# Attention's probabilities times values: 64 matmuls of one head, or 32 of two heads against block-diagonal values

## Chip, cores and metric

The kernel runs on one core of a Trainium2 chip. The metric is the time of one execution on the device, in microseconds (us), as the median of several runs. Durations of single instructions come from one profiled execution.

## What is computed

Two blocks, A (attention) and B (a gated MLP with a mix over positions), are applied twice, with the same weights. S is 2048, D is 576, there are 32 heads of 18.

```python
def _A_ref(x, wqkv, wo):                       # H = 32, Dh = 18, W = 8, dil = 2
    q, k, v = heads of (x @ wqkv)
    idx = pos[:, None] - off[None, :]          # off = 0, 2, ..., 14: eight keys, every second row back
    logits = where(idx >= 0, q . k[idx] * Dh ** -0.5, -1e9)
    o = softmax(logits) @ v[idx]
    return o (heads side by side) @ wo

def _B_ref(x, w_in, w_sp, b_sp, w_out):
    z1, z2 = halves of gelu(x @ w_in)
    g = w_sp @ layernorm(z2) + b_sp
    return (z1 * g) @ w_out

x = A_x
x = x + _A_ref(layernorm(x));  x = x + _B_ref(layernorm(x))
x = x + _A_ref(layernorm(x));  x = x + _B_ref(layernorm(x))
```

## The kernel before

Five phases follow one another. `phase_F(0)` normalizes x, does the first attention and the second half of the MLP's input projection. `phase_S(1)` does the first half of that projection and the mix over positions (`g_ps`). `phase_F(2)` first multiplies by `w_out` (`p_ps`), then does the second attention and projection as in the first; `phase_S(3)` mixes again and `phase_E` writes the result. The text calls `phase_F(0)` and `phase_F(2)` the first and second F stage. They hold all that the change touches.

Attention goes in 18 tiles of 114 queries with a halo of 14 rows before them. Since keys lie two rows apart, a tile's 128 rows are split by parity: 64 even and 64 odd rows never meet, and 57 queries of one parity see 64 keys of the same. For a tile t the steps are:

- `v{t}.m` (PE, 20 matmuls, `v_ps`): x times the value weights, 16 matmuls on 128x64 tiles of the array, 4 on 64x64 tiles for the last 64 of the 576 input features. Output rows are one parity each. `v{t}` copies the result, on ACT or DVE, into one of three buffers `v_ext`, which have a column of ones behind each head's 18.
- `a{t}.La`, `a{t}.L` (PE, 64 matmuls, `L_ps`): the scores, per head and parity 64 keys by 57 queries, four tiles of the array side by side.
- `a{t}.x0`, `.x1` (ACT): exp into `P`. `a{t}.k` (DVE) masks it.
- `a{t}.v` (PE, 64 matmuls, `O_ps`, L639), called PV below: for each head and parity the stationary operand is P, 64 keys by 64 (57 queries and 7 of padding), the moving one the head's 18 values and its one. Each sits on a 64x64 tile of the array.
- `a{t}.f` (DVE, L647 and L648): divide by the sum that the ones gave. Then `.t` (PE transpose, `o_tp`), `.e` (copy out), and per 128 rows the output projection `w_ps` (L695), the residual, a layernorm (its transposes are `ln_tp`, L325) and the MLP's projection `z_ps`.

The queries and keys come from `qk_ps` (45 matmuls for two tiles) and go through DRAM (`qk_bounce`) to get heads onto partitions.

Each F stage collects its steps in a `Flow`. A planner sorts them at build time: each step has an engine, a cost in us, a key, predecessors, and the buffers that it takes. PSUM tiles of two banks carry the tag "H", of which there are three, shared by `v_ps`, `L_ps`, `O_ps`, `qk_ps`, `w_ps`, `p_ps` and `z_ps`; a buffer is free again when the last step that uses it ends. The planner's order is then written into each engine's queue, and each engine works through its queue in that order. A step's `mode` names the way in which PE's array is tiled ("w" whole, "c" 128x64, "h" 64x64, "q" scores, "n" 64 rows); a step whose mode has two letters can begin in the one and end in the other. `pairs` counts a step's matmuls, with which the planner keeps a model of the fetching of PE's instructions. Keys and model have constants in `PLANS`, one `Plan` for each F stage.

```python
fl = Flow(dict(H=3, PT=2, QK=3, bn=2, stg=6, xt=NX, xn=3, ln_st=6, o_t=2), pl.STAY, self.pairs, pl.LF)
```

Of the kernel before, what the change touches and what calls it, by code (L numbers as in the profile page):

```python
# [18 lines left out]
P = 128  # L19
# [28 lines left out]
PLANS = (Plan(LX=4, LW=3.41, LR=3.7, KQ=4.43, KX=11.27,  # L48
              KV=1.9, KL=2.12, KE=20.8, KM=1.4, KP=2.05, KF=11.96, KY=2.1, KZ=15.77, KS=0.81, STAY=0.73, LF=4.38),
         Plan(LX=5.14, LW=3.5, LR=4.76, KQ=4.3, KX=10.56,  # L50
              KV=1.51, KL=1.98, KE=2.03, KM=0.75, KP=0.52, KF=4.06, KY=4.27, KZ=15.86, KS=0.39, STAY=0.48, LF=3.89))
# [140 lines left out]
class K:  # L192
# [219 lines left out]
    def phase_F(self, li):  # L412
# [14 lines left out]
        vb = [pool.tile([P, H, DH + 1], bf16, name=f"v_ext{k}") for k in range(3)]  # L427
        wqk = pool.tile([P, NM, 2 * D], bf16, name="wqk")
        wqk_r = pool.tile([P, D + HP], bf16, name="wqk_r")
        wv = pool.tile([P, NM, 2, 288], bf16, name="wv")  # L430
        wv_r = pool.tile([P, 288], bf16, name="wv_r")
# [45 lines left out]
        def load_v():  # L477
            self.load576(lambda s: wv[:, :, s, :], wv_r, self.A_wqkv[:, 2 * D:2 * D + 288],
                         self.A_wqkv[:, 2 * D + 288:3 * D], (nc.gpsimd if first else nc.sync,))
# [92 lines left out]
        def V_steps(t, key):  # L572
            box, v = {}, vb[t % 3]

            def mm(rest_first):
                ps = box["ps"] = self.Ht("v_ps")
                c0 = QT * t

                def part(first, wide):
                    for c in range(NM) if wide else (NM,):  # L580
                        for s in range(2):
                            rows = slice(0, P) if wide else slice(HP * s, HP * s + HP)
                            for par in range(2):
                                self.read_xn_strided(nc.tensor.matmul(  # L584
                                    ps[HP * (par ^ s):HP * (par ^ s) + HP, s, 0:288],
                                    lhsT=self.xnD[rows, c, c0 + par:c0 + P:2], rhs=wv[:, c, s, :] if wide else wv_r[rows, :],
                                    start=(first and c in (0, NM)), stop=(not first and c in (NM - 1, NM)),
                                    tile_position=(rows.start, HP * (par ^ s))), c0, c0 + P)
                part(True, not rest_first)
                part(False, rest_first)  # L590

            def ev(e):
                self.copy(e, v[:].rearrange("p (s b) d -> p s b d", s=2)[:, :, :, 0:DH],
                          box["ps"][:, :, 0:288].rearrange("p s (b d) -> p s b d", d=DH))
# [6 lines left out]
        def ATT_steps(t, key):  # L601
# [5 lines left out]
            def Lm(a):  # L607
                def f(_):
                    qk = self.QKs[group[t]]
                    ps = box["L", a] = self.Ht("L_ps")  # L610
                    for g in range(8):
                        for par in range(2):
                            for j in (2 * a, 2 * a + 1):
                                rows = slice(32 * j, 32 * j + DH)
                                at = HP * (par ^ (g // 4))
                                nc.tensor.matmul(ps[at:at + HP, j % 2, g * QH:(g + 1) * QH],  # L616
                                                 lhsT=qk[rows, g, 1, par, kb:kb + HP],
                                                 rhs=qk[rows, g, 0, par, kb + HALO // 2:kb + HALO // 2 + QH],
                                                 start=True, stop=True, tile_position=(32 * j, at))
# [13 lines left out]
            def pv(_):  # L633
                O = box["O"] = self.Ht("O_ps")
                for h in range(H // 2):
                    for s in range(2):
                        for par in range(2):
                            rows, to = slice(HP * (par ^ s), HP * (par ^ s) + HP), slice(HP * par, HP * par + HP)
                            nc.tensor.matmul(O[to, s, h * (DH + 1):(h + 1) * (DH + 1)],  # L639
                                             lhsT=Psb[rows, h % 4, h // 4 + 4 * s, :], rhs=v[rows, h + 16 * s, :],  # L640
                                             start=True, stop=True, tile_position=(rows.start, to.start))

            def fin(_):
# [14 lines left out]
            fl.step(tag + ".v", "PE", 0.75, key - pl.KP, pv, [tag + ".k", f"v{t}"] + ([f"a{t - 1}.v"] if t else []),  # L658
                    takes=[("H", tag + ".O")], mode="h", pairs=2 * H)
# [113 lines left out]
        def fills(part):  # L773
            if part == 0:
                for k in range(2):
                    nc.gpsimd.memset(Pb[k][:, :, :, QH:HP], 1.0)
                for k in range(3):
                    nc.gpsimd.memset(vb[k][:, :, DH:DH + 1], 1.0)
# [10 lines left out]
        fl.step("wo", q0, 1.2, -17, lambda _: load_o(), ["wv", "qk1"] if first else [], lag=4.0)  # L789
        fl.step("wzero", "POOL", 0.3, -19, lambda _: nc.gpsimd.memset(wqk_r[HP:P, NM * P:NM * P + P], 0.0))  # L790
        fl.step("fills", "POOL", 1.8, -16, lambda _: fills(0), ["wv", "lnx6.p"] if first else [])
# [185 lines left out]
```

## Time and profile before

| | us |
|---|---|
| runs | 1237.36, 1231.66, 1235.93 |
| median | 1235.93 |
| profiled execution | 1232.45 |
| its span, first to last instruction | 1230.8 |
| first F stage ends (first matmul of `phase_S(1)`) | 230.3 |
| second F stage (from its first `p_ps` to the first matmul of `phase_S(3)`) | 550.9 to 834.5 |

In rows of the profile, "PEld" is TensorE's load of a stationary operand and "PE" its matmul; "x64" is a count. A row of the timeline has its start and length in us, and in brackets how long the engine sat idle before it and what ended that. Consecutive instructions of a kind are merged, and a row's length reaches to the end of the last one's pipeline, so from one row's start to the next row's is the better measure of what a group costs.

### The profile page before, as it was taken

To read this page: it belongs to the slowest core of one execution; us is meant where nothing else is said; L and a number is where in the kernel's file an instruction comes from. 1 tells how busy PE (TensorE), PEld (TensorE's weight loads), DVE (VectorE), ACT (ScalarE), POOL (GpSimd) and SP (SyncE) were. 2 spreads that over 40 slices of the span, in tenths; PEclk is the share of its full clock that TensorE was granted. 3 is DMA by queue.
4 is the path that set the end of the run, shared out by engine and by line. 5 is a ranking of instruction groups with operands and counts; after the bars stand their busy time and mean duration, and the time that the engine had idled before them with its cause. 6 is when DMAs were issued, how large, how long until landed. Compare 5 with 4: busy or idle time off the path is not lost.

```text
span 1230.8 us, 27537 instructions
## 1 busy us (share of the span) xinstructions
PE 1195.9 (97%) x12032; PEld 680.9 (55%) x12094; DVE 531.5 (43%) x873; ACT 390.3 (32%) x667; POOL 198.9 (16%) x484
## 2 busy tenths in 40 slices
PE   6999999999999999999999999999999999999998
PEld 4676655444444444448777776554444444444576
DVE  6677765333232232333466666553232332232311
ACT  6664787510111111003344657772111001111000
POOL 6210267400000000002111114672000000000000
PEclk9999999999999999999999999999999999999999
DMA  7654346340000000032322362009300000000121
GB/s 201 131 131 118 75 96 133 75 96 2 10 10 10 10 11 1 1 108 86 74 62 57 92 160 56 17 22 263 94 10 10 1 10 10 10 1 29 40 68 49
DMA packets 140202, 75.09 MB, mean 61 GB/s; under 512 B 96576, under 2 KB 137216, under 8 KB 140080
## 3 DMA queue, kind: packets, MB, share of 16 engines
q1 hardware_dynamic: 139392, 70.94, 24.5%
q0 software_dynamic: 688, 2.38, 0.7%
q8 instruction: 95, 1.56, 0.6%
q14 instruction: 27, 0.22, 0.1%
HBM read 39.40 MB, written 17.11 MB: 46 GB/s over the span
## 4 chain that ended last, share of the span: by engine, by line
PE 93%; issue 2%; DMA 1%; ACT 1%; DVE 1%; SPq 1%; POOL 0%; ACTq 0%; POOLq 0%
PE g_ps L888 40%; PE p_ps L362 11%; PE z_ps L288 10%; PE z_ps L864 8%; PE qk_ps L288 5%; PE v_ps L584 4%; PE w_ps L695 3%; PE z_bank L864 3%; PE z_ps L282 2%; PE L_ps L616 2%; PE O_ps L639 2%; PE ln_tp L325 1%; PE z_ps L870 1%; PE qk_ps L282 1%; PE o_tp L667 1%
## 5 line engine op out<-in xcount | busy, mean ns | idle before, releaser
L888 PE MATMUL g_ps<-W,zu 128*128 128x512 bf16 x2256 | 497.7, 379 | 2.5
L888 PEld LDWEIGHTS <-zu 128*128 128x128 bf16 x2304 | 225.4, 98 | 271.8
L893 DVE TENSOR_TENSOR g_tmp<-g_ps,bsp 128x512 f32<-128x512 f32 x144 | 98.9, 687 | 432.9 <-PE g_ps L888 432.9
L880 ACT ACTIVATE zu<-z_ps 128x1024 bf16<-128x1024 f32 x54 | 51.4, 1024 | 515.9 <-PE z_ps L870 508.5
L362 PEld LDWEIGHTS <-zu 128*128 128x128 bf16 x1152 | 111.9, 98 | 31.0 <-DVE zu L894 2.1
L288 PE MATMUL z_ps<-wA,xnD 128*128 128x384 bf16 x576 | 109.8, 327 | 0.1
L362 PE MATMUL p_ps<-wA,zu 128*128 128x288 bf16 x768 | 105.9, 286 | 0.5 <-DVE ob L407 0.5
L894 DVE TENSOR_TENSOR zu<-g_tmp,zu 128x512 bf16<-128x512 f32 x144 | 99.6, 692 | 10.8
L288 PEld LDWEIGHTS <-xnD 128*128 128x128 bf16 x768 | 70.6, 98 | 56.2 <-issue 14.8
L864 PE MATMUL z_ps<-xnD,w 128*128 128x512 bf16 x424 | 95.8, 378 | 0.4
L864 PEld LDWEIGHTS <-w 128*128 128x128 bf16 x576 | 54.3, 97 | 71.8 <-issue 7.9
L732 ACT ACTIVATE zu<-z_ps 128x768 bf16<-128x768 f32 x96 | 77.2, 804 | 33.3 <-PE z_ps L288 17.4
L742 DVE CUSTOM_DVE_ANT_1 zu<-zu 128x1536 bf16<-128x1536 bf16 x32 | 56.6, 1770 | 49.1 <-ACT zu L732 49.1
L288 PE MATMUL qk_ps<-xnD,wqk 128*128 128x242 bf16 x576 | 73.4, 275 | 3.2 <-issue 2.1
L624 ACT ACTIVATE P<-L_ps 128x912 bf16<-128x912 f32 x72 | 64.7, 946 | 15.9 <-PE L_ps L616 14.4
L288 PEld LDWEIGHTS <-wqk 128*128 128x128 bf16 x576 | 54.0, 100 | 15.6 <-issue 9.5
L308 POOL TENSOR_SCALAR ln_st<-ln_st 128x1 f32<-128x1 f32 x64 | 15.4, 241 | 277.5 <-DVE ln_st L304 237.9
L319 ACT ACTIVATE xn<-zu,ln_st 128x512 bf16<-128x512 bf16 (+1 forms) x56 | 33.4, 647 | 66.0 <-POOL ln_st L310 65.7
L790 POOL MEMSET wqk_r<- 64x128 bf16 x2 | 0.4, 198 | 308.4 <-issue 308.4
L319 ACT ACTIVATE xn<-xt,ln_st 128x512 bf16<-128x512 bf16 x72 | 42.7, 648 | 20.1 <-POOL ln_st L310 20.0
L695 PE MATMUL w_ps<-wo,oT 128*128 128x288 bf16 x320 | 46.1, 293 | 2.7 <-ACT P L624 1.4
L288 PE MATMUL z_ps<-wB,xnD 128*128 128x384 bf16 x192 | 46.9, 326 | 0.0
(86 smaller groups left out, 1121.9 us busy)
## 6 DMA issues: line engine op xcount, KB each, us to landing
qk_bounce<-stg SPq DMA_DIRECT2D x72, 121.0 KB
QK<-qk_bounce SPq DMA_DIRECT2D x72, 121.0 KB
w<-in_B_w_in_dram SPq DMA_DIRECT2D x36, 128.0 KB
wA<-in_B_w_in_dram SPq DMA_DIRECT2D x12, 288.0 KB
wA<-in_B_w_out_dram SPq DMA_DIRECT2D x4, 864.0 KB
xres<-xt SPq DMA_DIRECT2D x18, 144.0 KB
x<-xres SPq DMA_DIRECT2D x16, 144.0 KB
out_dram<-ob SPq DMA_DIRECT2D x15, 144.0 KB
```

The costliest lines, as they stand in the source:

```text
L288: nc.tensor.matmul(ps(s), lhsT=lhsT, rhs=rhs, start=(c == 0 and not rest_first), stop=(c == NM - 1 and rest_first))
L319: nc.scalar.activation(out=out, in_=in_, func=ACT.Identity, scale=rstd[:n], bias=nmr[:n])
L362: nc.tensor.matmul(ps[:, hh, 0:288], lhsT=u[:, s * S + i * P:s * S + (i + 1) * P], rhs=wout(b, s)[:, hh * 288:(hh + 1) * 288], start=(b == ...
L624: nc.scalar.activation(out=Psb[:, 2 * hh:2 * hh + 2, :, 0:QH], in_=box["L", hh][:, :, 0:8 * QH].rearrange("p a (b c) -> p a b c", c=QH), f ...
L695: nc.tensor.matmul(box["ps"][:, hh, 0:288], lhsT=oT[:, c, at:at + P], rhs=wo[:, c, hh * 288:(hh + 1) * 288], start=(c == 0), stop=(c == 4))
L732: nc.scalar.activation(out=self.zu[:, 3 * u:3 * u + 3, 256 * i:256 * (i + 1)].rearrange("p j (s r) -> p s j r", s=2), in_=box[u][:, :, 0:3 ...
L742: nc.vector.tensor_tensor_reduce(out=junk(0, 6), in0=z[:, 0:6, :], in1=z[:, 0:6, :], scale=1.0 / FH, scalar=0.0, op0=ALU.mult, op1=ALU.add ...
L864: nc.tensor.matmul(out[q][h], lhsT=w1[:, NM * h + c, :], rhs=self.xnD[:, c, PADL + 512 * q:PADL + 512 * q + 512], start=(first and c == 0) ...
L880: nc.scalar.activation(out=uq, in_=H3[q][:], func=ACT.Gelu_apprx_tanh)
L888: nc.tensor.matmul(ps[:, s, :], lhsT=z2[:, i, s, :], rhs=W[q][:, i, :], start=(i == 0), stop=(i == NS - 1))
L893: nc.vector.tensor_tensor(out=tmp[:], in0=ps[:, s, :], in1=bsp[:, 512 * q:512 * (q + 1)], op=ALU.add)
L894: nc.vector.tensor_tensor(out=uv, in0=tmp[:], in1=uv, op=ALU.mult)
```

## The change

One PV matmul now takes two heads. Its stationary operand is P on all 128 rows, 64 keys of one head above 64 keys of another, same parity; its moving operand has 38 columns, 19 for each head, with zeros where the rows are the other head's (`v_ext` is block-diagonal and twice as wide). A matmul covers a 128x64 tile of the array, and there are 32 a tile instead of 64. For that

- the scores are written so that two heads of one parity lie above one another; their matmuls come in another order, number and size unchanged;
- `v_ps` has the even rows' heads and the odd rows' arranged anew (the weights are read as two runs of 144 columns), and is copied out in two steps of 64 rows, `v{t}.e0` and `v{t}.e1`, in place of one of 128 rows; PV waits for both;
- the three `v_ext` are zeroed at the start of each F stage (`vzero0` to `vzero2`, on DVE in the first, on POOL in the second), and the step `fills` waits for that;
- the value weights come in three DMAs in place of four;
- PV is entered in the planner with 0.45 us and 32 matmuls, not 0.75 and 64, and as mode "c", not "h"; the constants in `PLANS` are others, and so the order of all steps in both F stages is computed anew.

```diff
-PLANS = (Plan(LX=4, LW=3.41, LR=3.7, KQ=4.43, KX=11.27,
-              KV=1.9, KL=2.12, KE=20.8, KM=1.4, KP=2.05, KF=11.96, KY=2.1, KZ=15.77, KS=0.81, STAY=0.73, LF=4.38),
-         Plan(LX=5.14, LW=3.5, LR=4.76, KQ=4.3, KX=10.56,
-              KV=1.51, KL=1.98, KE=2.03, KM=0.75, KP=0.52, KF=4.06, KY=4.27, KZ=15.86, KS=0.39, STAY=0.48, LF=3.89))
+PLANS = (Plan(LX=4, LW=3.41, LR=3.7, KQ=4.95, KX=12.29,
+              KV=2.02, KL=2.15, KE=22.44, KM=1.86, KP=2.02, KF=13.34, KY=2.53, KZ=15.66, KS=0.73, STAY=0.73, LF=4.38),
+         Plan(LX=5.14, LW=3.5, LR=4.76, KQ=4.29, KX=10.53,
+              KV=0.36, KL=2.04, KE=1.11, KM=0, KP=0.18, KF=6.22, KY=4.16, KZ=15.99, KS=0.47, STAY=0.73, LF=3.89))
...
-        vb = [pool.tile([P, H, DH + 1], bf16, name=f"v_ext{k}") for k in range(3)]
+        vb = [pool.tile([P, 2, H // 2, 2, DH + 1], bf16, name=f"v_ext{k}") for k in range(3)]
...
             def ev(s):
+                def f(e):
+                    rows = slice(HP * s, HP * s + HP)
+                    self.copy(e, v[rows, :, :, s, 0:DH], box["ps"][rows, :, 0:288].rearrange("p r (h d) -> p r h d", d=DH))
+                return f
...
-            fl.step(f"v{t}", ("ACT", "DVE"), dict(DVE=0.78, ACT=0.66), key, ev, [f"v{t}.m"], [f"v{t}.ps"])
+            for s in range(2):
+                fl.step(f"v{t}.e{s}", ("ACT", "DVE"), dict(DVE=0.78, ACT=0.66), key, ev(s), [f"v{t}.m"], [f"v{t}.ps"])
...
-                    for g in range(8):
+                    for g in (0, 2, 1, 3, 4, 6, 5, 7):
...
-                                at = HP * (par ^ (g // 4))
-                                nc.tensor.matmul(ps[at:at + HP, j % 2, g * QH:(g + 1) * QH],
+                                at, to = HP * (g // 2 % 2), 4 * par + 2 * (g // 4) + g % 2
+                                nc.tensor.matmul(ps[at:at + HP, j % 2, to * QH:(to + 1) * QH],
...
-                for h in range(H // 2):
-                    for s in range(2):
+                for h in range(8):
+                    for b in range(2):
                         for par in range(2):
-                            rows, to = slice(HP * (par ^ s), HP * (par ^ s) + HP), slice(HP * par, HP * par + HP)
-                            nc.tensor.matmul(O[to, s, h * (DH + 1):(h + 1) * (DH + 1)],
-                                             lhsT=Psb[rows, h % 4, h // 4 + 4 * s, :], rhs=v[rows, h + 16 * s, :],
-                                             start=True, stop=True, tile_position=(rows.start, to.start))
+                            to = slice(HP * par, HP * par + HP)
+                            nc.tensor.matmul(O[to, b, 0:16 * (DH + 1)].rearrange("p (s h e) -> p s h e", s=2, h=8)[:, :, h, :],
+                                             lhsT=Psb[:, h % 4, 4 * par + 2 * b + h // 4, :], rhs=v[:, par, 8 * b + h],
+                                             start=True, stop=True, tile_position=(0, to.start))
...
-            fl.step(tag + ".v", "PE", 0.75, key - pl.KP, pv, [tag + ".k", f"v{t}"] + ([f"a{t - 1}.v"] if t else []),
-                    takes=[("H", tag + ".O")], mode="h", pairs=2 * H)
+            fl.step(tag + ".v", "PE", 0.45, key - pl.KP, pv, [tag + ".k", f"v{t}.e0", f"v{t}.e1"] + ([f"a{t - 1}.v"] if t else []),
+                    takes=[("H", tag + ".O")], mode="c", pairs=H)
...
+        vz = "DVE" if first else "POOL"
+        for k in range(3):
+            fl.step(f"vzero{k}", vz, 0.7 if first else 1.2, -21, lambda _, k=k: (nc.vector if first else nc.gpsimd).memset(vb[k][:], 0.0))
```

More of the change, by code (lines that the diff above doesn't have):

```diff
@@ L426, in phase_F @@
         wo = pool.tile([P, 5, D], bf16, name="wo")
-        vb = [pool.tile([P, H, DH + 1], bf16, name=f"v_ext{k}") for k in range(3)]
+        vb = [pool.tile([P, 2, H // 2, 2, DH + 1], bf16, name=f"v_ext{k}") for k in range(3)]
         wqk = pool.tile([P, NM, 2 * D], bf16, name="wqk")
         wqk_r = pool.tile([P, D + HP], bf16, name="wqk_r")
-        wv = pool.tile([P, NM, 2, 288], bf16, name="wv")
-        wv_r = pool.tile([P, 288], bf16, name="wv_r")
+        wv = pool.tile([P, NM, 2, 2, 144], bf16, name="wv")
+        wv_r = pool.tile([P, 2, 2, 144], bf16, name="wv_r")
         oT = pool.tile([P, 5, RING], bf16, name="oT")
@@ L477, in load_v @@
         def load_v():
-            self.load576(lambda s: wv[:, :, s, :], wv_r, self.A_wqkv[:, 2 * D:2 * D + 288],
-                         self.A_wqkv[:, 2 * D + 288:3 * D], (nc.gpsimd if first else nc.sync,))
+            eng = nc.gpsimd if first else nc.sync
+            self.dma(wv[:].rearrange("p c b s n -> p c (b s n)"),
+                     self.A_wqkv[0:NM * P, 2 * D:3 * D].rearrange("(c p) n -> p c n", p=P), eng)
+            for r in range(2):
+                self.dma(wv_r[HP * r:HP * r + HP].rearrange("p b s n -> p (b s n)"), self.A_wqkv[NM * P:D, 2 * D:3 * D], eng)
         def load_o():
@@ L777, in fills @@
                 for k in range(3):
-                    nc.gpsimd.memset(vb[k][:, :, DH:DH + 1], 1.0)
+                    for s in range(2):
+                        nc.gpsimd.memset(vb[k][HP * s:HP * s + HP, :, :, s, DH:DH + 1], 1.0)
                 nc.gpsimd.memset(wo[0:HP, 4, :], 0.0)
```

16 lines of the change are left out of this document (8 added, 8 removed).

## The prediction

> **What bounds the kernel now.** I read the page first, then who PE waited for, then stretches and the order of time around PE's longest pauses.
>
> ```profile
> PE 1195.9 (97%) x12032; PEld 680.9 (55%) x12094; DVE 531.5 (43%) x873; ACT 390.3 (32%) x667; POOL 198.9 (16%) x484
> q8 instruction: 95, 1.56, 0.6%
> ```
>
> PE is busy 97% of the span, so only two things can move the end: work that PE no longer does, and pauses of PE that go or come. The second row is the queue that brings instructions: 95 packets and 1.56 MB, 16.4 KB a packet. PE has 12032 + 12094 = 24126 instructions on the first row; 95 packets make 254 for each packet, about 127 pairs of a weight load and a matmul. The view of PE's waits shows what its pauses are:
>
> ```profile
> PE O_ps L639 <- issue: 4.1, 3, 2.0
> PE v_ps L584 <- issue: 3.8, 5, 1.8
> PE qk_ps L288 <- issue: 2.1, 3, 1.0
> PE w_ps L695 <- ACT P L624: 1.4, 1, 1.4
> PE L_ps L616 <- ACT P L624: 0.9, 1, 0.9
> PE L_ps L616 <- issue: 0.9, 1, 0.9
> PE O_ps L639 <- DVE zu L407: 0.7, 1, 0.7
> ```
>
> The figures are us in total, times, and the longest. "Issue" is a wait for nothing that the profile shows. The four such rows make 10.9 us; the w_ps row, 1.4, is put down to an exp that doesn't feed `w_ps`, so I count it with them: 12.3 us in all. The order of time from one pause to the next, PE alone, shows where they fall:
>
> ```profile
> 99.92 0.68 PE L639 MATMUL O_ps<-v_ext,P 64*64 64x19 bf16 x64
> 100.47 0.32 PE L584 MATMUL v_ps<-wv_r,xnD 64*64 64x288 bf16 x4
> 100.72 1.78 PE L584 MATMUL v_ps<-wv,xnD 128*64 128x288 bf16 x26
> 103.28 0.56 PE L584 MATMUL v_ps<-wv,xnD 128*64 128x288 bf16 x6 [0.77 <-issue]
> 103.77 0.32 PE L584 MATMUL v_ps<-wv_r,xnD 64*64 64x288 bf16 x4
> 104.02 0.70 PE L616 MATMUL L_ps<-QK 18*64 18x57 bf16 x64
> 104.65 0.45 PE L667 MATMUL o_tp<-ident,o_t 128*128 128x128 bf16 x5
> 104.94 0.44 PE L325 MATMUL ln_tp<-ident,xn 128*128 128x128 bf16 x5
> 105.22 0.99 PE L288 MATMUL qk_ps<-xnD,wqk 128*128 128x242 bf16 x8
> 106.14 0.38 PE L282 MATMUL qk_ps<-xnD,wqk_r 64*128 64x242 bf16 x4
> 106.46 1.83 PE L288 MATMUL qk_ps<-xnD,wqk 128*128 128x242 bf16 x16
> 108.22 0.28 PE L282 MATMUL qk_ps<-xnD,wqk_r 64*128 64x242 bf16 x2
> 108.43 1.23 PE L639 MATMUL O_ps<-v_ext,P 64*64 64x19 bf16 x128
> 109.49 0.31 PE L584 MATMUL v_ps<-wv_r,xnD 64*64 64x288 bf16 x4
> 109.74 0.81 PE L584 MATMUL v_ps<-wv,xnD 128*64 128x288 bf16 x10
> ```
>
> Both pauses cut a V step in its middle (26 and 10 matmuls in), where no operand is missing. From 103.28 to the second pause stand 6+4+64+5+5+8+4+16+2+128+4+10 = 256 matmuls: two packets exactly. Stretches between ends of pauses (length, PE's busy time and matmuls, granted clock, DMA) say the same:
>
> ```profile
> 40.03:44.94 4.91, 3.86 (x127) 1.00 0.43 136
> 44.94:49.58 4.64, 3.76 (x127) 1.00 1.03 154
> 725.02:741.33 16.31, 14.18 (x382) 1.00 0.61 154
> ```
>
> 127, 127 and 382 (three times 127). So PE pauses where a packet of its own program ends and the next isn't there; starved, it gets one packet in 4.64 to 4.91 us. I call such a packet a block of 128 matmuls. Elsewhere a block holds 128 long matmuls and the fetch is hidden; in attention it can hold 2 us of work.
>
> The Trainium skill, in "Runtime: NRT & Kernel Launch" (Instruction fetch mechanics), has the instruction memory refilled in 16 KiB blocks of 256 instructions, and calls the cost of crossing a block mostly hidden. The trace agrees on the block (254) and disagrees on the cost (12.3 us); by that rule the next part's first two terms would be nothing, a rival below.
>
> Two pauses have an aftermath. The granted clock (the figure behind the matmuls) after them:
>
> ```profile
> 112.20:115.62 3.42, 3.24 (x19) 0.50 0.02 5
> 132.68:136.10 3.42, 3.19 (x14) 0.50 0.46 88
> ```
>
> Half the clock for 3.42 us costs 1.7 us twice, 3.4 us. Pauses of the fetch thus cost 12.3 + 3.4 = 15.7 us, all in the two F stages.
>
> **The change part by part.**
>
> *Fewer instructions.* PV has 64 matmuls a tile and gets 32; 36 tiles lose 1152 pairs, 9 blocks. What counts is the blocks that hold too little work. I price a matmul by the rows above, from its start to the next group's start: scores 0.63/64 us, PV 1.06/128, V (0.25 for four, 1.78/26 for the rest) 0.067 on average, transposes 0.0575, projection 0.92/8. The output projections, 128 columns of weights and 288 of data, come from
>
> ```profile
> 554.00 1.63 PE L362 MATMUL p_ps<-wA,zu 128*128 128x288 bf16 x12
> 555.47 0.90 PE L362 MATMUL p_ps<-wB,zu 128*128 128x288 bf16 x6
> ```
>
> as 1.47/12 = 0.1225. With these prices I go through the order in which each kernel's PE instructions are built, in blocks of 128, and add up what each block lacks to 4.64 us. I do it for four places where the first block may begin and average. Before: 17.7 us lacking in the first F stage and 20.7 in the second, 38.4; after, with PV at double the price a matmul, 7.6 and 8.3, 15.9; with PV at the old price 19.7. That is no time, since blocks fetched ahead make up for part of it, but the ratio is what I use: 0.41 of the lack stays (0.51 at most), so of 12.3 us of pauses 5.1 stay: **-7.2 us** (bounds: nothing, if the pauses have another cause, and -12.3). No long pause, no half clock: two windows of 1.7 us; I expect three quarters to go, **-2.5** (0 to -3.4).
>
> *PV itself.* 1.06 us for 128 matmuls is 0.53 a tile. Four array tiles of 64x64 work side by side, so 16 rounds of 33 ns. The new matmuls cover 128 rows, so only two (left and right 64 columns) stand side by side: 32 matmuls are again 16 rounds. What sets a round? Not the data: 57 columns in the scores (0.63/64, four tiles as well) cost 39 ns a round against 33 for 19. It looks like the load of 64 weight columns, and that doesn't depend on rows:
>
> ```profile
> L584 PEld LDWEIGHTS <-xnD 128*64 128x64 bf16 x576 | 30.7, 111 | 11.2 <-issue 6.7
> L639 PEld LDWEIGHTS <-P 64*64 64x64 bf16 x2304 | 22.2, 109 | 9.2 <-issue 7.1 <-DVE P L631 0.2 <-DVE stg L342 0.2
> ```
>
> 111 ns for 128 rows against 109. So a PV step stays near 0.53. If a matmul costs 8.3 ns wherever it runs, it falls to 0.27: 36 x 0.26 = -9.4 us. If load and 38 data columns didn't overlap in a tile, a round grows by the 38 columns (1.78/26 for 288 columns in two tiles is 137 ns a round, so 18 ns): 16 x 18 ns x 36 = +10 us. The V steps, with the same 128x64 tiles, do overlap (137 ns a round with a load in it). I take **-0.9**, by the scores' and V's rows. Changes of tile size on PE are as many in the new order (179 in the first stage; 179 against 186 in the other).
>
> The skill's "TensorEngine Tiling (Array Packing)" (Instruction Overhead) says that a matmul of one column takes as long as one of 60. The rows lean to it (39 against 33 ns). By itself it would make half the matmuls half the time, but it leaves out that half the tiles stand side by side; the sum by it is the second rival.
>
> *Two evacuations of V for one.* Each takes 64 rows, but 576 elements in each row as the whole did, so I give each the whole's time. Copies, then busy times of PE, its loads, DVE, ACT and POOL in two stretches:
>
> ```profile
> L343 ACT CAST v_ext<-v_ps x28: 627/641/653, 25.4 to 758.5; 128x576 bf16<-128x576 f32 x28
> L342 DVE CAST v_ext<-v_ps x8: 707/759/760, 24.0 to 747.1; 128x576 bf16<-128x576 f32 x8
> 35.00:150.00 115.00, 106.17 (x3014) 81.77 (x3012) 83.09 (x150) 69.50 (x106) 19.36 (x44) 0.97 0.52 118
> 575.00:785.00 210.00, 202.66 (x4011) 151.83 (x4009) 129.50 (x233) 117.17 (x193) 50.87 (x122) 1.00 0.33 76
> ```
>
> The built order gives DVE 33 halves for 8 wholes (25 x 0.76 = 19 us more) and ACT 39 for 28 (11 x 0.64 = 7 us more). DVE has 115 - 83 = 32 us free in the first attention stretch and gets 16 halves there, 12 us; the other stretch has 80 free on DVE, 93 on ACT. So the work has room. The price is lateness: `v_ps` holds one of three "H" slots until both halves are out, and PV now waits for both. Behind a late half on PE stand the next score or projection matmuls that need the slot; the mask and the normalization on DVE stand behind the copy. I take **+2.5** (0 to 25, if each tile's half were in PE's way).
>
> *Zeroing the values.* Three memsets of 1216 bf16. In the first stage on DVE ahead of the first statistics:
>
> ```profile
> 0.91 0.09 DVE L226 MEMSET xnD<- 128x35 uint32 x1
> 0.95 0.07 DVE L227 MEMSET xnD<- 128x10 uint32 x1
> 3.06 0.46 DVE L303 BATCH_NORM_STATS2 ln_st<-zu 128x6 f32<-128x288 bf16 x1 [2.05 <-DMA zu<-in_A_x_dram]
> ```
>
> 25 words more cost 0.02 us; 608 words then 0.55 us, three 1.65, inside the 2.05 that DVE waits for x: **0**. Were it per bf16 element (1.04 each), 1.1 us would stick out, straight on the path to the first matmul. In the second F stage POOL does them ahead of its layernorm steps, under the p_ps matmuls (rows of 554 us) that come first: 0. The value weights come by one DMA less on POOL's and SP's queues; rows and x loads behind it go up by an issue, nothing on the path: 0.
>
> *Scores and V matmuls* keep number, size and tiles; scores visit the same two tiles twice running, then the other two. With loads pulled ahead that costs nothing; the V weights are read in two runs of 144: 0.
>
> **Sum.** 1232.45 (profiled execution, span 1230.8) - 7.2 - 2.5 - 0.9 + 2.5 = 1224.3. The timed median, 1235.93, is 3.5 above the profiled execution; I add half of that and forecast **1226 us**. Its own range is 1220 (the other pauses and their half clock gone too, 5.1 and 0.9) to 1232 (half of the gain on pauses fails, 3.6, and the evacuations cost 2.5 more).
>
> **The rivals.**
>
> *PV halves as well.* 8.3 ns is then a cost of each matmul. For it: 39 ns against 33 with thrice the columns, so columns count little. Against: rounds with few tiles (V) show no gain from fewer matmuls. 1226 + 0.9 - 9.4, and 1.2 back because blocks get emptier: 1219. Chance 0.15.
>
> *The pauses aren't worth anything.* Crossing a block is hidden by other work, or the pauses move to other places of the new order; the first two terms vanish: 1226 + 9.7 = 1236, no change. The skill's rule of the fetch is this case. Against it: counts of 127, 256 and 382. Chance 0.15, with PV at +10 us in it (1236 too).
>
> *The second half of V's evacuation is in PE's way.* In-order ACT and DVE put it behind an exp or a mask; PE lacks a slot. From (7.2 + 2.5 + 0.9)/36 = 0.29 us a tile on, the change loses; at 0.70 a tile (the mean of 0.64 and 0.76) it is 25 us: 1226 - 2.5 + 25 = 1248.5, slower. For it: DVE goes from 83 to 95 of 115 us in the first stretch. Against: in the waits above ACT and DVE hold scores and PV up by 0.9 and 0.7 us in all. Chance 0.22.
>
> **How the numbers follow.** The forecast has 0.48. A measurement of this kernel can tell about 0.5% from no change, here 6.2 us: below 1229.8 is faster, above 1242.1 slower. Of the forecast's 0.48 I put 0.43 below 1229.8, with 0.15 of the first rival: 0.57 with rounding. No change: 0.05, 0.13 of the second rival, little of the third: 0.20. Slower: 0.23. The range, 1213 to 1246, reaches from the first rival with its other pauses gone (0.51 x 12.3 = 6.3 us) to the third at 0.63 us a tile.
>
> **What would show it.** Right: the instruction queue has some 86 packets (95 - 9); PE's waits on "issue" at O_ps, v_ps, qk_ps and L_ps make 5 us or less; no window at half clock in attention; a PV step of 32 starts its successor 0.5 us on. Wrong: PV at 0.27 or 0.8 us a step; pauses of PE that DVE or ACT end, in rows of O_ps, L_ps and qk_ps, of over 10 us; pauses on "issue" as long as before.

## The result, and the profile after

The changed kernel takes 1226.88 us, median of 6 runs (1225.88 to 1229.43), beside 1233.14 for the kernel before (1230.36 to 1237.36, also 6): ratio 0.9939, 95% interval 0.9918 to 0.996. It is faster by some 6 us. The profiled execution took 1226.56 us, its span 1224.8. From the page of after, the engines' busy times and the queue that brings instructions:

```profile
PE 1196.8 (98%) x10942; PEld 679.3 (55%) x10942; DVE 551.4 (45%) x894; ACT 396.8 (32%) x683; POOL 200.4 (16%) x492
...
q8 instruction: 86, 1.41, 0.5%
```

86 packets, as forecast. PE's busy time hardly moved (1195.9 before, where 62 matmuls are missing in the records: 12094 loads, 12032 matmuls); its idle time fell from 1230.8 - 1195.9 = 34.9 to 28.0 us, though 2.5 us of the 34.9 are gaps at `g_ps`, where 48 of the missing records are. What the idle time is now, by the view of PE's waits (us in total, times, the longest):

```profile
PE ln_tp L325 <- ACT xn L319: 9.7, 3, 8.0
PE L_ps L624 <- DMA QK<-qk_bounce: 2.3, 5, 0.7
PE w_ps L703 <- DVE v_ext L342: 1.5, 4, 0.5
...
PE O_ps L647 <- DVE v_ext L342: 1.4, 4, 0.4
...
PE qk_ps L288 <- DVE v_ext L342: 1.0, 3, 0.5
PE L_ps L624 <- DVE v_ext L342: 0.7, 1, 0.7
...
PE p_ps L362 <- DVE v_ext L342: 0.6, 2, 0.3
...
PE qk_ps L288 <- ACT v_ext L343: 0.5, 1, 0.5
...
PE L_ps L624 <- issue: 0.5, 1, 0.5
PE O_ps L647 <- ACT v_ext L343: 0.2, 1, 0.2
```

The waits for nothing, 12.3 us before, are down to one of 0.5. In their place stand seven rows in which PE waits until a copy into `v_ext` ends, 5.9 us together; before there was none. Only two of them are PV (`O_ps`). The others are `w_ps`, `qk_ps`, `L_ps` and `p_ps`, which read no values: they wait for an "H" slot of PSUM that `v_ps` holds. The order of time on PE shows the longest such wait, and three stretches (length, busy times, granted clock, DMA) what follows from it:

```profile
136.65 0.69 PE L647 MATMUL O_ps<-v_ext,P 128*64 128x38 bf16 x32
137.27 0.45 PE L624 MATMUL L_ps<-QK 18*64 18x57 bf16 x32
137.65 0.45 PE L675 MATMUL o_tp<-ident,o_t 128*128 128x128 bf16 x5
...
139.13 0.55 PE L624 MATMUL L_ps<-QK 18*64 18x57 bf16 x32 [0.75 <-DVE v_ext L342]
140.31 0.73 PE L624 MATMUL L_ps<-QK 18*64 18x57 bf16 x64 [0.63 <-DVE o_t L656]
...
141.27 4.29 PE L703 MATMUL w_ps<-wo,oT 128*128 128x288 bf16 x20
```

```profile
32.30:35.70 3.40, 3.40 (x61) 2.21 (x51) 2.32 (x5) 3.40 (x5) 2.86 (x7) 0.52 0.32 69
141.60:145.00 3.40, 3.40 (x17) 2.07 (x16) 3.13 (x5) 2.21 (x4) 1.43 (x3) 0.51 0.02 5
...
35.00:150.00 115.00, 108.02 (x2502) 83.01 (x2502) 92.07 (x160) 73.64 (x116) 16.46 (x42) 0.98 0.54 120
```

The score step at 139.13 waited 0.75 us for a copy, the next one 0.63 us for DVE, and from 141.6 on PE ran at half clock for 3.4 us. Two windows at half clock are left of three. A PV step of 32 matmuls starts its successor 137.27 - 136.65 = 0.62 us on, a change of tile size included; over all 36 the median is 0.53 (0.61 before), worked out from the starts in the records. That is not a cheaper step: in both kernels an undisturbed step is 0.53 us where the next group keeps the tile size and 0.61 or 0.62 where it changes, and 26 steps of after have a group of the same tile size behind them, 18 before. In the stretch from 35 to 150 us PE works 1.85 us longer than before and waits that much less, though it now holds 2502 recorded matmuls and not 3014.

The first stage's beginning went the other way:

```profile
3.77 1.07 DVE L801 MEMSET v_ext<- 128x1216 bf16 x1 [0.20 <-issue]
...
8.00 0.72 PE L325 MATMUL ln_tp<-ident,xn 128*128 128x128 bf16 x5 [8.00 <-ACT xn L319]
```

Each of the three memsets takes 1.07 us, and the first matmul starts at 8.00; before it was 6.37.

### The profile page after: what moved, and what is told of

It reads as the page before. It is cut to its first block, busy times and chain, and to the rows that moved or that the text cites. A ratio compares the mean times of both kernels' runs of the same rounds, so it can differ in the third digit from the quotient of the medians.

```text
span 1224.8 us, 25328 instructions
## 1 busy us (share of the span) xinstructions
PE 1196.8 (98%) x10942; PEld 679.3 (55%) x10942; DVE 551.4 (45%) x894; ACT 396.8 (32%) x683; POOL 200.4 (16%) x492
## 4 chain that ended last, share of the span: by engine, by line
PE 91%; DVE 3%; DMA 2%; ACT 1%; POOL 1%; SPq 1%; issue 1%; POOLq 0%; DVEq 0%
PE g_ps L900 41%; PE p_ps L362 11%; PE z_ps L288 11%; PE z_ps L876 8%; PE qk_ps L288 4%; PE w_ps L703 3%; PE v_ps L588 3%; PE z_bank L876 3%; PE z_ps L282 2%; PE O_ps L647 2%; DVE v_ext L342 1%; PE z_ps L882 1%; ACT v_ext L343 1%; PE ln_tp L325 1%; DMA QK<-qk_bounce 1%; PE qk_ps L282 1%
## 5 line engine op out<-in xcount | busy, mean ns | idle before, releaser
L308 POOL TENSOR_SCALAR ln_st<-ln_st 128x1 f32<-128x1 f32 x64 | 19.5, 304 | 273.9 <-DVE ln_st L304 226.3
L801 POOL MEMSET v_ext<- 128x1216 bf16 x3 | 3.2, 1107 | 301.5 <-PE g_ps L900 301.5
```

## The experiments

Each kernel was timed in turn with the kernel before on the same chip; ratios are to that. The changed kernel is "after"; unless said otherwise a variant differs from it by the diff shown and PE's order of steps is the same.

### The price of a PV step by itself

After the last matmul of after stand eight probes, each behind 24 long matmuls:

```diff
+        run(64, 64, 64, 19, q4)       # matmuls, rows, weight columns, data columns, tiles side by side
+        run(32, 128, 64, 38, c2)
+        run(32, 128, 64, 19, c2)
+        run(32, 128, 64, 76, c2)
+        run(32, 128, 32, 38, c2)
+        run(64, 64, 64, 57, q4)
+        run(32, 128, 128, 38, [(0, 0)])
+        run(32, 128, 64, 38, [(0, 0)])
```

> The changed kernel with eight series of matmuls behind its last one, on a PE that is warm and waits for nothing; series are parted by 24 whole-array matmuls of 512 columns. Their results go to no output. Price of a series, from its first start to the next group's first start. Theory A, a round of the array's side-by-side tiles costs the load of its weight columns (33 ns for 64) whatever rows and data there are: 64 of 64x64 with 19 columns on four tiles 0.53 us; 32 of 128x64 on two tiles 0.53 us with 19, with 38 and with 76 columns; 32 of 128x64 on one tile 1.06 us; 32 weight columns in place of 64 nearly half, 0.27 to 0.35; 64 of 64x64 with 57 columns 0.53. Theory B, every matmul has its 8.3 ns wherever it runs: 32 matmuls 0.27 us in all series of 32, 0.53 in those of 64. Theory C, load and data don't overlap in a tile: 0.53 with 19 columns, 0.66 with 38, 0.9 with 76.

From the timeline of this kernel, PE alone:

```profile
1225.43 0.68 PE L946 MATMUL probe<-zu 64*64 64x19 bf16 x64
1226.04 5.35 PE L940 MATMUL probe<-zu 128*128 128x512 bf16 x24
1231.32 0.68 PE L946 MATMUL probe<-zu 128*64 128x38 bf16 x32
1231.94 5.35 PE L940 MATMUL probe<-zu 128*128 128x512 bf16 x24
...
1243.12 0.74 PE L946 MATMUL probe<-zu 128*64 128x76 bf16 x32
1243.79 5.35 PE L940 MATMUL probe<-zu 128*128 128x512 bf16 x24
1249.08 0.57 PE L946 MATMUL probe<-zu 128*32 128x38 bf16 x32
1249.58 5.35 PE L940 MATMUL probe<-zu 128*128 128x512 bf16 x24
...
1260.69 0.96 PE L946 MATMUL probe<-zu 128*128 128x38 bf16 x32
1261.50 5.34 PE L940 MATMUL probe<-zu 128*128 128x512 bf16 x24
```

From start to start, the old PV step takes 0.61 us and the new one 0.62; with 19 data columns 0.61, with 76 it is 0.67. So 16 rounds cost the same whether they hold 64 matmuls or 32, and hardly ask how many columns stream. With 32 weight columns it is 0.50. The forecast's account of PV stands, except for one thing: half the weight columns don't halve it.

### The new order and work, with the old PV

```diff
-  nc.tensor.matmul(O[to, b, ...], lhsT=Psb[:, ...], rhs=v[:, par, 8 * b + h], tile_position=(0, to.start))
+  for s in (par, 1 - par):
+      r = slice(HP * s, HP * s + HP)
+      nc.tensor.matmul(O[to, s, ...], lhsT=Psb[r, ...], rhs=v[r, par, 8 * b + h, s], tile_position=(r.start, to.start))
```

> The changed kernel with its own order of steps on every engine, both evacuations of V and the zeroing, but each PV matmul of 128 rows is issued as two of 64 rows on 64x64 tiles: 64 a tile again, 1152 more pairs of PE instructions, the same rounds of the array. Fetch theory: the pauses where a block of PE's program ends come back, 6 to 12 us, and the time goes to 1233 to 1239, no faster than before the change. Order theory (the gain is the new order of steps): it stays at 1227. Rival that PV itself became cheaper: PV's steps take longer by 0.2 us each, 8 us, without pauses.

Two things go with it: the four matmuls of V on 64x64 tiles stand at the other end of their step, beside PV's matmuls, which are on tiles of that size again, and DVE's division reads its sums in another order (it takes 0.757 us as in after).

1237.14 us (1233.06 to 1240.91), ratio 1.0023 [1.0004, 1.0043]: 10.2 us over after, and no gain left. PE's waits, and one of the five stretches at half clock:

```profile
PE L_ps L625 <- issue: 5.3, 6, 1.9
...
PE w_ps L707 <- issue: 2.0, 1, 2.0
PE O_ps L650 <- issue: 1.8, 2, 0.9
```

```profile
754.00:760.80 6.80, 6.80 (x129) 4.46 (x126) 4.33 (x8) 4.23 (x6) 1.05 (x3) 0.50 0.08 24
```

A PV step costs PE the same either way, so those 10.2 us are the fetching of the 1152 pairs: waits for nothing are back (9.1 us in these rows) and PE is at half clock for longer (20.5 us, against 6.8 in after). From each of the last five of these pauses to the next (689.66, 704.61, 719.41, 737.26 and 752.67 us) stand 382 matmuls in the records, three packets as in the kernel before. This shows the theory of the fetch at its own place: the order of steps and the copies are the same, and the number of PE's instructions differs.

### Without the second half of V's copy

This kernel leaves out half of the values; it serves for its time alone.

```diff
-                    self.copy(e, v[rows, :, :, s, 0:DH], ...)
+                    if s == 0:
+                        self.copy(e, v[rows, :, :, s, 0:DH], ...)
```

> The changed kernel with the second evacuation of V left out (the heads of V's odd rows' half stay zero); order of all else unchanged. If the second half is in PE's way, the waits of PE that copies into v_ext end (1.5, 1.4, 1.0, 0.7, 0.6, 0.5 and 0.2 us in the rows of the changed kernel, 5.9 in all) shrink to under 2 us and the time falls by 4 to 6 us, to 1221 to 1223. If PE would have waited at those places for something else, the time stays within 1.5 us of 1227.

1213.68 us (1213.23 to 1214.71), ratio 0.984 [0.9813, 0.9868]: 13.2 us under after, where 4 to 6 were expected. From its page:

```profile
PE 1190.3 (98%) x10942; PEld 676.2 (56%) x10942; DVE 532.5 (44%) x870; ACT 387.9 (32%) x671; POOL 200.2 (17%) x492
```

Its span is 1212.2. PE idles 21.9 us, 6.1 less than in after, about what the rows of `v_ext` hold (other waits come and go: those for the fetch are 2.3 us here). It is also busy for 6.5 us less; the two windows at half clock, which this run did not have, account for 3.4 of that.

### The old order with the new work

The planner's constants and its entries for PV and V are those of the kernel before; both halves go as one step, on one engine, and the zeroing goes as in the next experiment.

```diff
-    fl.step(f"v{t}.e{s}", ("ACT", "DVE"), ..., ev(s), ...)
+    fl.step(f"v{t}", ("ACT", "DVE"), ..., lambda e: [ev(s)(e) for s in range(2)], ...)
-    fl.step(tag + ".v", "PE", 0.45, ..., mode="c", pairs=H)
+    fl.step(tag + ".v", "PE", 0.75, ..., mode="h", pairs=2 * H)
```

> The order of steps of the kernel before, on every engine, with the work of the changed one: PV as 32 matmuls of 128 rows, both halves of V copied out one behind the other on the same engine in the place of the one copy, zeroing at the start. Fetch theory: pauses of PE on issue fall from 12 us to 5 us or less though no order is computed anew; with the second halves (2 to 8 us) the time is 1226 to 1233. Order theory: without the new order nothing is gained and the halves cost, 1236 to 1242.

1228.92 us (1227.64 to 1239.23), ratio 0.9966 [0.9944, 0.9988]. By the ratios the work alone brings 0.34% of the 0.61%, a little over half, and the new order the rest; the two intervals overlap, so the share is not shown closely. Two waits for the fetch are left in it:

```profile
PE L_ps L626 <- issue: 2.2, 2, 1.3
```

### Zeroing as words

```diff
-  vb = [pool.tile([P, 2, H // 2, 2, DH + 1], ...)]
+  vf = [pool.tile([P, 2 * H * (DH + 1)], ...)]          # vb is a view of it
-  (nc.vector if first else nc.gpsimd).memset(vb[k][:], 0.0)
+  (nc.vector if first and k < 2 else nc.gpsimd).memset(vf[k][:], 0.0)
```

> The changed kernel; the tiles of the values are flat, so that their zeroing runs on words of 4 bytes (608, not 1216 elements), and in the first F stage two of the three are on DVE and one on POOL. If the zeroing ahead of the first statistics is what moved PE's first instruction from 6.37 to 8.00 us, it comes back to 6.4 to 6.6 us and the time falls by 1.4 to 1.7 us, to 1225.3. If the start is hidden by the loads behind it, PE's first instruction comes sooner and the time stays at 1226.9.

1226.93 us (1225.71 to 1228.37), ratio 0.9946 [0.9929, 0.9963]. From its timeline:

```profile
1.09 1.21 DVE L802 MEMSET v_ext<- 128x608 uint32 x2
...
6.29 0.71 PE L325 MATMUL ln_tp<-ident,xn 128*128 128x128 bf16 x5 [6.29 <-ACT xn L319]
```

The start is back to 6.29 and the time is the same. The first F stage ends 2.3 us sooner (225.6 against 227.9) and the second is 1.5 us longer (281.4 against 279.9). This execution has more half clock: one at 742.7 us, and one at 29.3 us that lasts 6.8 us and not 3.4, each losing 1.7 us more. So the zeroing's 1.6 us is there to see but can't be told in the time.

### Old order in the first stage, new in the second

The first stage is that of the kernel with the old order (it ended its first stage at 224.75 us, after at 227.89), the second that of after.

> First F stage with the order of steps of the kernel before (as in e5_old_order, where it ended at 224.75 us against 227.89 in the changed kernel), second F stage with the changed kernel's order (279.94 us long there, against 285.08 in e5_old_order); work of the changed kernel in both. If the stages are independent, 1226.9 less 3.1 us: 1223 to 1225. If the second stage depends on where the blocks of PE's program fall after the first, which this keeps as in the changed kernel, or on what the first leaves behind, it is 1226 or more.

1226.47 us (1225.15 to 1232.67), ratio 0.9942 [0.9925, 0.996]. The first stage ended at 225.09, as hoped; the second took 281.53, not 279.94, with a window at half clock (741.7 us) that after doesn't have there. No gain over after.

### On which engine the halves are copied

Two kernels, both with zeroing as words: all halves on ACT, or the first on ACT and the second on DVE, in hope of having them side by side.

```diff
-   self.copy(e, v[rows, ...], ...)
+   self.copy("ACT", v[rows, ...], ...)                   # the one
+   self.copy(("ACT", "DVE")[s], v[rows, ...], ...)       # the other
```

> e4_zero with all halves of V copied by ACT, put in its queue where the order has them (DVE had 33 of 72). If the price of the second half is DVE's lateness, the waits of PE that v_ext ends (5.9 us in the changed kernel) fall to 2 us or less and the time to 1220 to 1223. If the price is the length of two copies one behind the other while PSUM is held, the waits stay, under ACT's name, and the time stays at 1225 or rises.

> e4_zero with the first half of each tile's V always on ACT and the second always on DVE, put in their queues where the order has them. Length theory: side by side, the two take 0.76 us and not 1.4 to 1.5, waits that v_ext ends fall to 3 us or less, the time to 1221 to 1224. Lateness theory: DVE's half still comes late, as often as before, and nothing is gained against e4_zero.

1226.96 us (ratio 0.9947 [0.9923, 0.997]) and 1228.54 (0.9954 [0.9937, 0.997]): neither helps. With all on ACT, PE's waits for a copy stay, under ACT's name:

```profile
PE w_ps L704 <- ACT v_ext L343: 2.3, 5, 0.9
...
PE qk_ps L288 <- ACT v_ext L343: 1.9, 4, 0.9
```

So a busy DVE isn't the cause. With a half on each engine, the timeline of a pair:

```profile
48.26 0.64 ACT L343 CAST v_ext<-v_ps 64x576 bf16<-64x576 f32 x1 [0.60 <-PE v_ps L589]
48.92 0.76 DVE L342 CAST v_ext<-v_ps 64x576 bf16<-64x576 f32 x1 [0.77 <-ACT v_ext L343]
```

They are not side by side. DVE sat idle for 0.77 us and began when ACT's half was out (48.26 + 0.64 = 48.90). The same stands in after, in the view of the tile `v_ps` (durations: shortest, median, longest; then what ended the idle time of its users, us and times):

```profile
L343 ACT CAST v_ext<-v_ps x39: 627/633/698, 42.3 to 747.6; 64x576 bf16<-64x576 f32 x39
L342 DVE CAST v_ext<-v_ps x33: 694/764/765, 25.8 to 740.8; 64x576 bf16<-64x576 f32 x33
...
  ACT v_ext L343: 13.6, 18
  DVE v_ext L342: 2.8, 3
```

In 21 tiles of 36 the second half waited for the first on the other engine; in two more the engines differ and the second came later by itself, and in 13 both halves are on one engine. They overlap in none. The built program holds that wait: in all 23 tiles of after with two engines, and in all 36 of the kernel with one half on each, the second copy waits for a semaphore that the first one's engine raises. Either way `v_ps` keeps its slot for two copies in a row, 1.43 us in the median of after, where one copy took 0.63 to 0.76 before. The Trainium skill, in "PSUM — Partial Sum Buffer" (PSUM bank collisions raise a hardware error), says that two engines may use a bank at once if their rows lie in different quadrants, as these halves do. No run here shows that, and a version without the wait wasn't tried.

### The slot, PV's wait, or the load?

Three kernels tell apart what the second copy costs. In the first it reads SBUF and no longer `v_ps`; in the second it writes `v_ps` onto itself, and PV doesn't wait for it; in the third it is left out again, with 0.25 in the value tiles where they held zeros. All three leave out half of the values, or have other numbers in their place, and serve for their times alone.

```diff
+   src = box["ps"][rows, :, 0:288] if s == 0 else wqk[rows, 0, :].bitcast(f32)...      # from SBUF
+   self.copy(e, v[rows, :, :, s, 0:DH] if s == 0 else src, src)                        # in place
+   if s == 0: self.copy(...)    and    memset(vb[k][:], 0.25)                          # filled
```

> The second half of V is copied from a stretch of the query and key weights in SBUF, read as f32 (576 elements a row), not from v_ps: so it still takes its engine as long and PV still waits for it, but it no longer holds v_ps. It leaves out the values of the second half. If what costs is the slot that v_ps holds, the 13 us go as without the copy: 1214, and PE's waits that a copy into v_ext ends fall from 5.9 to 1 us. If PV's wait for the second half costs, or the load on the two queues: 1224 to 1227, with the waits at O_ps still there. If the zeros in the values' second half were what made the kernel without that copy fast (its matmuls draw less), this one, whose second half isn't zero, stays at 1224 to 1227 with half-clock windows and no waits for the copies.

> The second half is copied out of v_ps onto itself: the copy takes its engine as long and holds v_ps as long, but PV doesn't wait for it. It leaves out the values of the second half, which stay zero. Slot: 1225 to 1227, waits for the copies still at L_ps, qk_ps and w_ps. PV's wait: 1214 to 1217. Load on the queues: 1225 to 1227. Zeros in the values: 1214 to 1219.

> The second half of V is not copied, as in the run that left it out, and the value tiles start at 0.25 where they started at zero, so that PV's moving operand has no zeros. If the zeros made that run fast: 1217 to 1221 with windows at half clock back. If not, 1214 with none, as there; then all of the 13 us come from the second copy itself.

| second copy | us | ratio | span times granted clock, us |
|---|---|---|---|
| as in after | 1226.88 | 0.9939 [0.9918, 0.996] | 1220.5 |
| in place, PV doesn't wait | 1226.90 | 0.9942 [0.9922, 0.9962] | 1218.6 |
| from SBUF, PV waits | 1215.36 | 0.9851 [0.983, 0.9871] | 1210.1 |
| none, values filled | 1215.18 | 0.9841 [0.9823, 0.9859] | 1210.1 |
| none | 1213.68 | 0.984 [0.9813, 0.9868] | 1210.4 |

The last column is the median over a kernel's executions of its span times its mean granted clock. It estimates the time with the half clock taken out, good to about 1 us; a window that falls where PE waits anyway costs less than it counts.

The second copies of the kernel that reads SBUF, from the view of `v_ext`:

```profile
L342 DVE CAST v_ext<-wqk x24: 458/460/461, 26.2 to 729.5; 64x576 bf16<-64x576 f32 x24
...
L343 ACT CAST v_ext<-wqk x12: 728/730/733, 41.9 to 736.5; 64x576 bf16<-64x576 f32 x12
```

And of the one in place, from the view of `v_ps`:

```profile
L342 DVE COPY v_ps<-v_ps x24: 775/776/777, 26.0 to 739.4; 64x576 f32<-64x576 f32 x24
L343 ACT COPY v_ps<-v_ps x12: 615/615/615, 41.8 to 747.9; 64x576 f32<-64x576 f32 x12
```

PE's waits of the one in place, where nothing reads what the second copy writes:

```profile
PE w_ps L704 <- DVE v_ps L342: 1.7, 4, 0.5
PE O_ps L648 <- DVE v_ps L342: 1.6, 5, 0.4
```

It is the slot: with the copy holding `v_ps` and nothing waiting for its result, the whole time is there, and even the waits at `O_ps` are, so those too are for a slot; with the copy on the same engines and PV waiting for it, but `v_ps` free, next to nothing is. By the last column the slot costs 8.5 of 10.4 us and PV's wait 2 at most; the times differ by more, 11.5 to 13.2 us, because after is at half clock for longer. (From SBUF, DVE's copy is shorter by 0.3 us; ACT's is longer by 0.1.) One more thing differs between these two: from SBUF the two halves no longer wait for one another, and overlap in 21 tiles, so an engine isn't held up behind the other's half. That this is not the price is seen in the kernel with all halves on ACT, which has no such wait and takes 1226.96 us. Nor do zeros in the values make a run fast. The filled kernel was at half clock for 6.8 us, as long as after, and is fast all the same, so the clock isn't the cause either. Its page row, for a span of 1212.2:

```profile
PE 1193.0 (98%) x10942; PEld 677.9 (56%) x10942; DVE 533.1 (44%) x870; ACT 387.6 (32%) x671; POOL 203.2 (17%) x492
```

PE idles 19.2 us here, 8.8 less than in after, and is busy 3.8 less. Part of that busy time is how waits are counted: a row reaches to the end of its last matmul's pipeline, and the wait behind it is counted from there. In the rows of after shown above, five transposes at 0.058 us from 137.94 on could have been followed at 138.23; the score step came at 139.13, 0.90 us late, of which 0.75 are shown. Matmul by matmul in the records (both kernels have the same 10942 in the same order), after loses 8.2 us at its 16 waits for `v_ext`, 6.1 of them shown as idle; so 2 of the 3.8 us are waits. The other 4.4 of the 12.6 us between the two spans are spread over waits for `QK` (1.7), for other results of DVE and ACT, and pauses too short for a row; why those grow when a slot is late is open.

### One copy out of PSUM, then a move

What the three point to: let one copy take all 128 rows out of `v_ps`, and sort out the second half's place in SBUF, on DVE. Zeroing at the start goes as words here, which by itself changed no time.

```diff
+   if "out" not in box:
+       box["out"] = s
+       self.copy(e, v[:, :, :, 0, 0:DH], box["ps"][:, :, 0:288].rearrange(...))
+   else:
+       nc.vector.tensor_copy(out=v[HP:P, :, :, 1, 0:DH], in_=v[HP:P, :, :, 0, 0:DH])
+       nc.vector.memset(v[HP:P, :, :, 0, 0:DH], 0.0)
```

> All 128 rows of V leave v_ps in one copy again (so it holds its slot for one copy of 0.64 to 0.76 us, as in the kernel before), into the first of the two places that a pair of heads has in a row; DVE then moves the 64 rows that belong in the second place, inside SBUF, and zeroes where they stood. The zeroing at the start goes as 608 words. PE's order is that of the changed kernel. By the theory of the slot: what the second copy costs goes, 13 us, less what PV's later start costs (the move and the zeroing, together some 0.8 us a tile on DVE, none of it holding a slot): 1213 to 1217, with no waits of PE that a copy into v_ext ends, but for up to 2 us at O_ps. If the work on DVE (36 x 0.8 us against 33 halves of 0.76) or the later PV cost as much as the slot: 1224 to 1228 with waits at O_ps.

1219.31 us (1216.76 to 1222.85), ratio 0.9869 [0.9844, 0.9894], on another chip, where the kernel before takes 1235.75: faster than after, and the intervals don't meet. From the view of `v_ext`:

```profile
L604 DVE COPY v_ext<-v_ext x36: 356/361/405, 25.1 to 740.0; 64x576 bf16<-64x576 bf16 x36
L605 DVE MEMSET v_ext<- x36: 298/298/298, 25.6 to 740.4; 64x288 uint32 x36
L343 ACT CAST v_ext<-v_ps x27: 639/641/647, 54.1 to 739.3; 128x576 bf16<-128x576 f32 x27
```

In PE's waits `v_ext` ends only one of 0.3 us. By the times the gain is 7.6 us of the 13.2, less than expected (1213 to 1217); by the ratios, which allow for the chip, it is 8.6 of 12.2. The first stage ends at 220.93, 7 us sooner than in after, but the second took 279.73, where it was 276.3 without the second copy. Most of the rest is half clock and the chip: the profiled execution has 10.2 us of it, 5.1 lost, where the kernel without the second copy had none. Span times granted clock, it is at 0.988 of the kernel before on its chip (1212.4 of 1226.7), the same as the kernel without the second copy on the other (1210.4 of 1224.7), though with a start that is 1.6 us sooner.

## Why the prediction was right, and where it was wrong

The forecast was 1226.0, its own range 1220 to 1232; measured were 1226.88. That they agree to 0.9 us is in good part luck. The sum forecast a fall of 8.1 us, from a base (the profiled execution and half of the way to a median of three, 1235.93) that six executions put 1 us lower, at 1233.14; the profiled executions differ by 5.9 us, the medians by 6.3. And the terms were off by more than that, with opposite signs:

- **Fewer instructions, -7.2: right in kind, too small.** By the same view, waits for nothing fell from 12.3 to 0.5 us, so 11.8, close to the bound of 12.3. The step that failed is "0.41 of the lack stays": the lack that remained became almost no pause. (The `w_ps` row was rightly counted in: from the pause at 112.38 us to it stand 508 matmuls, four packets of 127. V's price, 1.78/26, has the pipeline's tail in it: the 26 starts lie 0.060 us apart.) That blocks fetched ahead make up for many small lacks is the likely reason, but it wasn't shown. With the order kept, the 1152 pairs are worth 10.2 us, the half clock included.
- **Half clock, -2.5: 1.7.** One window of three went. One in attention was forecast to go and didn't: it now follows waits for `v_ext` and `o_t`. Whether a pause is followed by a window isn't settled by its length alone: in the kernel before, pauses of 1.83 and 1.36 us have one behind them, those of 1.71 and 2.02 us (at 725 and 741 us) have none.
- **PV itself, -0.9: right.** 0.61 and 0.62 us by themselves. What PV gains in the kernel is fewer steps with a change of tile size behind them, 0.09 us each for eight steps. The rival that PV halves (the first of the rivals, though the prediction once calls it the second) falls. So does the rule of the Trainium skill's "TensorEngine Tiling (Array Packing)" (Instruction Overhead), if the price that it gives a matmul of few columns is read as one to be paid for each of several side by side: 64 and 32 matmuls cost the same.
- **Two evacuations, +2.5: the term that was mis-sized; it is 11.5 to 13.2,** by the kernels whose second copy leaves `v_ps` alone or is left out, half clock included. "Work has room" was right: load on DVE and ACT cost next to nothing, and PV's wait 2 us at most. The slot was named too, held "until both halves are out", but priced near the low end of its bounds, by the waits of before, in which a slot held for one copy hardly hurt. Held for two copies in a row it costs 0.32 to 0.37 us a tile (of 36). The third rival's mechanism is thus what happened, above its own point of decision (0.29 us a tile); the change still wins because what the fetch gave back was larger than the 10.6 us which that point was worked out from: without the second copy the kernel is 1233.14 - 1213.68 = 19.5 us faster than before, with fetch, half clock and the new order in it. It was also missed that halves on two engines wait for each other.
- **Zeroing, 0: wrong at its place.** The choice of words (0.55 us each) failed: the tile's innermost run of 19 bf16 isn't a whole number of words, so the memsets ran per element, 1.07 us each with 0.2 between, and the first matmul came 1.6 us later. The bound given, 1.1, left out those gaps. The Trainium skill, "VectorE: DVE Perf Modes" (Zero memsets can be issued as uint32), has one cycle per element whatever the type, and a word form only for whole words; 1.07 us for 1216 elements and 0.6 for 608 words agree that the time goes by elements and not by bytes; the length of a cycle is not read here.
- **The pauses aren't worth anything** (the second rival): refuted by the kernel with the old PV, which loses all of the gain.

These terms don't add up to the measured change: -11.8 - 1.7 - 0.9 + 13.2 is -1.2, and the profiled executions differ by -5.9. Where the other 4.7 us come from is not shown. Two things may be in them: a pause costs some 0.15 us more than its row shows, by the rows above, which makes some 2 us for the 12 pauses that went (an estimate); and the new order of steps, for which the sum has no term, and without which the kernel takes 2.0 us more (1228.92).

Of the signs named: packets 86, waits on "issue" below 5 us and PV's 0.53 came as said; the half clock in attention did not go; the pauses that copies end are 5.9 us, under the 10 named as a sign of the third rival, and still its price was 11.5 to 13.2. A wait's rows understate what a late slot costs.

## What to carry to other kernels

Where two short copies replace one long copy out of PSUM, ask how long the buffer is held, not whether the engines have time: here the engines had it and the slot cost 0.32 to 0.37 us a tile. Empty PSUM in one instruction and rearrange in SBUF. Where PE stops in the middle of a step with every operand there, count the instructions between stops; if they come in one fixed number, fewer instructions are worth more than shorter ones; here half as many matmuls of the same total time gave back 10.2 us.

## What was not expected of the hardware

- A round of matmuls on tiles side by side costs by its weight columns, but not in proportion: from first to last start, worked out from single records of the probes, 33 ns with 64 weight columns (0.499 us for 15 steps), 26 with 32 (0.390), and 25 for a matmul of 128x128 by itself (0.779 for 31). Twice 64 columns side by side thus take longer than 128 in one.
- Windows at half clock last 3.4 us, or 6.8 where two follow one another, and come and go between kernels whose PE order is the same (and between executions of one kernel: the mean granted clock of after's six goes from 0.994 to 0.997): none without the second copy, 6.8 us of them in after (3.4 us lost), 20.5 with the old PV (10.2 lost). The Trainium skill, "TensorE: Matmul & The Clock Gate" (Part 1), has a window of 3413 ns that runs free of the kernel; the trace agrees on the length.
